# Splitting the output projection's weight of a decode block into nine groups, six of them gathered with different partitions left out

## The chip, the cores and the metric

The kernel runs on one core of one Trainium2 chip. The metric is device time in microseconds (us) of one execution; the number that counts is the median of several runs. Everything below that is called a profile or a trace is one profiled execution of the same program.

## What is computed

The reference is one decode step of a transformer block: two tokens (B = 2, one position each, D = 512), attention over a cache of 8192 keys and values for 32 heads of 128, and an MLP.

```python
# x [2,1,512]; k_cache, v_cache [2,32,8192,128]; wq [512,4096]; wo [4096,512]; w1 [512,1792]; w2 [1792,512]
q = layernorm(x) @ wq                       # 32 heads of 128
p = softmax(q . k_cache * 128**-0.5)        # per token and head, over 8192 positions
o = p . v_cache                             # [2, 32*128]
h = x + o @ wo
out = h + gelu(layernorm(h) @ w1 + b1) @ w2 + b2
```

The two caches are 268 MB each in float32 and are read once. All other operands together are about 25 MB; `wo`, which the change is about, is 8.4 MB.

## The kernel before

**Units of work.** Two heads of one token make a unit: 32 units, `i = 0 .. 31`, where unit `i` is head pair `m = i // 2` and token `b = i % 2`. A unit has one tile of keys and one of values, 4 MB each: 128 partitions (64 for each head) by 128 positions by 128 values. The tiles come from one pool, `kv`, with three buffers, in the order k0, v0, k1, v1, ..., so the load of `v_i` has to wait until `k_(i-1)` is used up, and that of `k_(i+1)` until `v_(i-1)` is. All these loads are issued by SyncE (SP), in that order (L65).

**One unit.** The scores are made in four chunks. VectorE (DVE) multiplies the key chunk by the query in place (L219, 4.4 us each), then sums part of the rows (L227), while ScalarE (ACT) sums the others (L223). After the fourth chunk `row_max` takes the largest score of each partition (L231), TensorE (PE) turns it, and at the start of the next unit `all_max` finds the largest of each head (L238, tile `gm`). From it ACT makes the exponentials (L254), and PE multiplies them with the values (L279). So DVE's work on unit `i` ends with the `gm` instruction, and the next thing on its queue is the first multiply of unit `i + 1`, which needs the keys `k_(i+1)`.

**The output projection.** `wo` of the first 30 heads, 3840 rows of 2 KB, is used in groups. A group is a tile `wog` of 128 partitions by 4 rows (`wts` pool, one buffer), loaded ahead by `load_wo`. `head_out` scales the finished head outputs and lays them out as the tile `orow` asks (L314), `turn` transposes that on PE (L322), `turned` copies it (L329, DVE) and multiplies it with `wog` into `rowacc` (L331, PE). The next group is loaded in the unit after that (`free_from`). The last two heads have their own load and path at the end.

**Two ways to load a group.** A plain group fills all 128 partitions with one DMA issued by SP (L125). A gathered group has 448 rows, 112 runs of 4 rows. GpSimd (POOL) fills the tile with zeros (L129) and issues an indirect DMA (L130) with one index for each partition; the partitions in `SHUT` get an index beyond the bounds and are left out. Before, there are four gathered groups, all with the same 16 partitions left out, and then four plain ones.

**The indices.** They are worked out on DVE, one set for each distinct tuple of blocks:

```python
index = {}
for blocks in SHUT:
    if blocks not in index:
        acc = work.tile([P, 1], F32, name="ixf")
        nc.vector.tensor_copy(acc, part)
        for s0 in blocks:
            for edge, step in ((s0, FAR), (s0 + 4, -FAR - 4)):
                one = work.tile([P, 1], F32, name="ix1")
                ...
        index[blocks] = const.tile([P, 1], I32, name="ix")
        nc.vector.tensor_copy(index[blocks], acc)      # L112
```

**What orders the work.** The tile framework keeps the order of each engine's queue near the order in the code (a few places say `behind(...)`), and adds the waits. A pool gives every name its own buffers, `const` one for each name, `work` two, `kv` three. A tile that is allocated under a name again takes the buffer of an earlier one, after what last used that one.

Of the kernel before, what the change touches and what calls it, by code (L numbers as in the profile page):

```python
# [16 lines left out]
P = 128  # L17
# [6 lines left out]
WARM = 3  # L24
WR = 4

SHUT = [(0, 4, 32, 36)] * 4
FAR = 4096


# [1 line left out]
def tile_decode_block(ctx: ExitStack, tc: tile.TileContext, x, k, v, wq, wo, w1, b1, w2, b2, out):  # L32
    nc = tc.nc
    B, H, SK, DH = k.shape
    D = x.shape[-1]
# [40 lines left out]
    def next_of_pool(make):  # L76
        with tc.issue_after(pool[0].ins):
            pool[0] = make()
# [2 lines left out]


    HL = H - QG
    GR = (P - 16) * WR
    groups = [(GR * g, GR, WR) for g in range(len(SHUT))]
    at = groups[-1][0] + GR
    while at < HL * DH:
        r = min(WR, (HL * DH - at) // P)
        groups.append((at, r * P, r))
        at += r * P  # L90
    kept = [[p for p in range(P) if g >= len(SHUT) or not any(s <= p < s + 4 for s in SHUT[g])]
            for g in range(len(groups))]
    group_end = {}
    for g, (r0, n, r) in enumerate(groups):
        group_end.setdefault((r0 + n - 1) // (QG * DH), []).append(g)

    part = const.tile([P, 1], F32, name="part")
# [1 line left out]
    next_of_pool(lambda: nc.gpsimd.iota(parti, [[0, 1]], base=0, channel_multiplier=1))  # L99
    nc.vector.tensor_copy(part, parti)  # L100
    index = {}
    for blocks in SHUT:
        if blocks not in index:
            acc = work.tile([P, 1], F32, name="ixf")
            nc.vector.tensor_copy(acc, part)
            for s0 in blocks:
                for edge, step in ((s0, FAR), (s0 + 4, -FAR - 4)):
                    one = work.tile([P, 1], F32, name="ix1")
                    nc.vector.tensor_scalar(one, part, edge - 0.5, float(step), op0=ALU.is_ge, op1=ALU.mult)
                    nc.vector.tensor_add(acc, acc, one)  # L110
            index[blocks] = const.tile([P, 1], I32, name="ix")
            nc.vector.tensor_copy(index[blocks], acc)  # L112
# [4 lines left out]
    wo_runs = wo.rearrange("(m r) n -> m (r n)", r=WR)  # L117
    wo_g = {}

    def load_wo(g, gate=None):  # L120
        r0, n, r = groups[g]
        t = wts.tile([P, WR, D], F32, name="wog")
        wo_g[g] = t
        if g >= len(SHUT):
            nc.sync.dma_start(t[:, :r], wo[r0:r0 + n, :].rearrange("(p r) n -> p r n", r=r))  # L125
            return
        if gate is not None:
            next_of_pool(lambda: nc.gpsimd.tensor_copy(gate0, gate))
        next_of_pool(lambda: nc.gpsimd.memset(t, 0.0))  # L129
        next_of_pool(lambda: nc.gpsimd.indirect_dma_start(  # L130
            t.rearrange("p r n -> p (r n)"), None, wo_runs, bass.IndirectOffsetOnAxis(index[SHUT[g]], 0),
            element_offset=r0 * D, bounds_check=P - 17, oob_is_err=False))

    epst = const.tile([P, 1], F32, name="epst")
    nc.vector.memset(epst, EPS)
# [167 lines left out]

    def head_out(h):
        rl = RL[h // QG * B + B - 1][:, h % QG:h % QG + 1]
        for g, (r0, n, r) in enumerate(groups):
            a, end = max(r0, h * DH), min(r0 + n, (h + 1) * DH)
            while a < end:
                q = (a - r0) // r
                run = 1  # L310
                while a + run * r < end and kept[g][q + run] == kept[g][q] + run:
                    run += 1
                c0, p0 = a - h * DH, kept[g][q]
                nc.vector.tensor_scalar(orow[g % 2][:B, :r, p0:p0 + run].rearrange("b r p -> b p r"),  # L314
                                        OP[h // QG][:, h % QG, c0:c0 + run * r].rearrange("b (p r) -> b p r", r=r),
                                        rl, None, op0=ALU.mult)
                a += run * r

    def turn(g):
        TP[g] = psm.tile([P, WR, B], F32, name="sm")  # L320
        for r in range(groups[g][2]):
            nc.tensor.transpose(TP[g][:, r, :], orow[g % 2][:B, r, :], ident[:B, :B])  # L322
        if g + 2 < len(SHUT) and SHUT[g + 2] != SHUT[g]:
            next_of_pool(lambda: nc.gpsimd.memset(orow[g % 2][:B], 0.0))

    def turned(g):
# [18 lines left out]
    for i in range(NI):  # L345
# [24 lines left out]
        if next_load < len(groups) and i == free_from:  # L370
            load_wo(next_load, MX[i - 1][:1, 0:1] if next_load == 0 else None)
            next_load += 1
            free_from = NI
        for c in range(NC):
            if i > 0 and c == 0:
                with behind(last):
                    mul = multiply(i, c)
            else:
                mul = multiply(i, c)
            ended = [g for g in group_end.get(done // B, ())] if done >= 0 and done % B == B - 1 else []  # L380
            with behind(mul):
                if i > 0 and c == 1:
                    inverse(done)
                if i > 0 and c == 2 and done % B == B - 1:
                    for h in range(done // B * QG, done // B * QG + QG):
                        head_out(h)
                if c == 3:
                    for g in ended:
                        turned(g)
                        free_from = i + 1  # L390
            by_act(i, c)
            if i > 0 and c == 0 and not late:
                gather(done)
            by_dve(i, c)
            if i > 0 and c == 0:
                total(done)
            if i > 0 and c == 1 and not late:
                head_sum(done)
            if c == 2:
                for g in ended:  # L400
                    turn(g)
# [154 lines left out]
```

## Time and profile before

| what | value |
|---|---|
| median of three runs | 1315.71 us (1313.37 to 1316.23) |
| the profiled execution: its own time | 1317.28 us |
| its span, first to last instruction | 1315.5 us |
| DMA: moved in all, mean rate | 561.67 MB, 427 GB/s |
| DVE busy | 971.2 us, 74% of the span |
| ACT busy | 479.4 us, 36% |
| PE busy | 459.0 us, 35% |
| POOL busy | 12.8 us, 1%, 18 instructions |
| granted TensorE clock, mean | 0.662 |

The span is what the views of the trace count in; the execution's own time is 1.8 us longer, and 1.6 us above the median. The page gives busy time for each engine, the DMA share in 40 slices, the chain of work that ended last, and groups of instructions by line. A timeline line reads: start, time from there to the end of the last instruction in the line, engine, line, operation, tile written and tiles read, count, and in brackets how long the engine sat idle before it and what ended that. L12 is line 12 of the kernel. In the changed kernel the lines named here are one higher (L112 becomes L113, L219 becomes L220).

### The profile page before, as it was taken

To read this page: it belongs to the slowest core of one execution; us is meant where nothing else is said; L and a number is where in the kernel's file an instruction comes from. 1 tells how busy PE (TensorE), PEld (TensorE's weight loads), DVE (VectorE), ACT (ScalarE), POOL (GpSimd) and SP (SyncE) were. 2 spreads that over 40 slices of the span, in tenths; PEclk is the share of its full clock that TensorE was granted. 3 is DMA by queue.
4 is the path that set the end of the run, shared out by engine and by line. 5 is a ranking of instruction groups with operands and counts; after the bars stand their busy time and mean duration, and the time that the engine had idled before them with its cause. 6 is when DMAs were issued, how large, how long until landed. Compare 5 with 4: busy or idle time off the path is not lost.

```text
span 1315.5 us, 10328 instructions
## 1 busy us (share of the span) xinstructions
PE 459.0 (35%) x3231; PEld 147.0 (11%) x3231; DVE 971.2 (74%) x447; ACT 479.4 (36%) x2955; POOL 12.8 (1%) x18
## 2 busy tenths in 40 slices
PE   3024213342332324313442332424412244323438
PEld 0001001110110101001010010101001011011104
DVE  1766788767788676788776788767688677798991
ACT  0333344433344333344333344333344333344441
POOL 0000000000000000000000000000000000000000
PEclk9566557766666667656766566766657676556758
DMA  9999999999999999999999999999999999999996
GB/s 415 443 417 441 422 439 439 423 437 430 433 435 425 439 431 429 431 430 437 431 427 437 435 427 435 425 439 435 425 437 430 435 433 425 439 423 423 442 415 263
DMA packets 13470, 561.67 MB, mean 427 GB/s; under 512 B 1556, under 2 KB 1572, under 8 KB 2984
## 3 DMA queue, kind: packets, MB, share of 16 engines
q1 hardware_dynamic: 12828, 557.34, 98.3%
q0 software_dynamic: 576, 3.67, 0.7%
q8 instruction: 25, 0.41, 0.1%
q14 instruction: 29, 0.24, 0.0%
q10 hardware_dynamic: 12, 0.01, 0.0%
HBM read 561.53 MB, written 0.00 MB: 427 GB/s over the span
## 4 chain that ended last, share of the span: by engine, by line
DMA 44%; DVE 32%; PE 17%; issue 6%; ACT 1%; POOL 0%; DVEq 0%; SPq 0%; POOLq 0%
DMA kv<-in_A_k_cache_dram 44%; DVE kv L219 21%; PE so L279 11%; DVE s L227 9%; PE rowacc L331 4%; ACT pt L254 1%; DVE orow L314 1%; PE so L501 0%; PE sm L242 0%; PE po L524 0%; PE sm L234 0%; DVE gm L238 0%; PE sm L484 0%; DVE mx L231 0%; ACT nb L248 0%
## 5 line engine op out<-in xcount | busy, mean ns | idle before, releaser
L219 DVE TENSOR_TENSOR kv<-kv,qps 128x4096 f32<-128x4096 f32 x128 | 560.7, 4411 | 277.5 <-DMA kv<-in_A_k_cache_dram 277.5
L223 ACT ACTIVATE kv<-kv 128x128 f32<-128x128 f32 x1376 | 403.9, 295 | 335.3 <-DVE kv L219 335.3
L227 DVE TENSOR_REDUCE s<-kv 128x20 f32<-128x2560 f32 (+2 forms) x128 | 377.7, 2972 | 0.3
L279 PE MATMUL so<-kv,pt 128*8 128x512 f32 x2048 | 284.3, 713 | 55.1 <-ACT pt L254 36.5
L223 ACT ACTIVATION_READ_ACCUMULATOR kv<-kv 128x1 f32 x1376 | 256.7, 187 | 0.0
L234 PE MATMUL sm<-ident,mx 128*1 128x128 f32 x32 | 11.1, 346 | 315.5 <-DVE mx L231 315.5
L285 ACT ACTIVATE ss<-so 128x512 f32<-128x512 f32 x32 | 19.1, 597 | 280.0 <-PE so L279 149.7
L204 PE MATMUL qps<-q,pick 2*64 2x128 f32 x128 | 16.7, 409 | 283.6 <-DVE kv L219 283.6
L279 PEld LDWEIGHTS so<-kv,pt 128*8 128x8 f32 x2048 | 58.3, 101 | 250.6 <-issue 208.7
L248 ACT ACTIVATE nb<-sm 128x1 f32<-128x1 f32 x32 | 5.5, 171 | 169.1 <-PE sm L242 169.1
L331 PE MATMUL rowacc<-wog,ot 128*2 128x512 f32 x64 | 47.4, 911 | 52.7 <-issue 27.1
L300 PE MATMUL sm<-ss,selr 128*2 128x128 f32 x480 | 55.8, 275 | 0.7 <-ACT ss L285 0.7
L204 PEld LDWEIGHTS qps<-q,pick 2*64 2x64 f32 x128 | 10.9, 202 | 297.4 <-DVE kv L219 274.4
L322 PE MATMUL sm<-ident,orow 2*128 2x2 f32 x32 | 4.5, 241 | 105.1 <-DVE orow L314 105.1
L300 PEld LDWEIGHTS sm<-ss,selr 128*2 128x2 f32 x480 | 39.2, 85 | 13.7 <-ACT ss L285 1.7
L234 PEld LDWEIGHTS sm<-ident,mx 128*1 128x1 f32 x32 | 2.5, 79 | 332.1 <-issue 287.5
L238 DVE TENSOR_REDUCE gm<-sm 1x2 f32<-1x128 f32 x32 | 8.9, 279 | 30.8 <-PE sm L234 30.8
L254 ACT ACTIVATE pt<-s,nb 64x128 f32<-64x128 f32 x64 | 25.5, 399 | 1.6 <-ACT nb L248 0.2
L331 PEld LDWEIGHTS rowacc<-wog,ot 128*2 128x2 f32 x64 | 6.6, 111 | 86.2 <-issue 60.3
L322 PEld LDWEIGHTS sm<-ident,orow 2*128 2x128 f32 x32 | 4.0, 209 | 107.3 <-issue 78.8
L242 PE MATMUL sm<-gm,srow 1*64 1x1 f32 x128 | 11.2, 238 | 11.5 <-DVE gm L238 11.5
L191 PE MATMUL so<-wqs,yT 128*2 128x512 f32 x64 | 9.2, 742 | 15.0 <-DMA wqs<-in_A_wq_dram 15.0
(100 smaller groups left out, 126.1 us busy)
## 6 DMA issues: line engine op xcount, KB each, us to landing
kv<-in_A_k_cache_dram SPq DMA_DIRECT2D x4, 4096.0 KB
kv<-in_A_k_cache_dram SPq DMA_DIRECT2D x4, 2048.0 KB, 26.5
wog<-in_A_wo_dram SPq DMA_DIRECT2D x4, 1024.0 KB, 36.3
kv<-in_A_v_cache_dram SPq DMA_DIRECT2D x1, 4096.0 KB, 36.0
ws<-in_B_w_dram SPq DMA_DIRECT2D x4, 896.0 KB, 10.8
kv<-in_A_v_cache_dram SPq DMA_DIRECT2D x1, 2048.0 KB, 40.5
ws<-in_B_w_dram SPq DMA_DIRECT2D x2, 1024.0 KB
kv<-in_A_v_cache_dram SPq DMA_DIRECT2D x1, 1536.0 KB
```

Source lines behind the costliest of these rows:

```text
L204: nc.tensor.matmul(qps[m][e * HP:(e + 1) * HP, b], pick[32 * n:32 * n + B, b, :], q2[32 * n:32 * n + B, at + e * DH:at + (e + 1) * DH], st ...
L219: return nc.vector.tensor_tensor(kc, kc, qb, op=ALU.mult)
L223: nc.scalar.activation(kt[i][:, j, :], kt[i][:, j, :], AF.Copy, accum_out=ST[i][:, j:j + 1])
L227: return nc.vector.tensor_reduce(ST[i][:, a:e], kt[i][:, a:e, :], axis=AX.X, op=ALU.add)
L234: nc.tensor.transpose(MT[i], mx, ident)
L242: nc.tensor.matmul(GM[i][e * HP:(e + 1) * HP], srow, gm[:, e:e + 1], start=True, stop=True)
L254: nc.scalar.activation(ptz[i % 2][ps, :, 4 * e:4 * e + 4], s[ps], AF.Exp, bias=nb[ps], scale=SCALE, accum_out=LT[m][ps, b:b + 1])
L279: m = nc.tensor.matmul(so[32 * n:32 * n + 4 * QG], ptz[i % 2][:, u, :], vt[i][:, 4 * u:4 * u + 4, :], start=(u < NG), stop=(u >= NS // 4 - ...
L285: return nc.scalar.activation(SS[i], so2[i % 2], AF.Copy)
L300: nc.tensor.matmul(OP[m][:, e, :], sel_row[:, c, 4 * e + j, :], SS[i - 1 + c][:, j * DH:(j + 1) * DH], start=(c == 0 and j == 0), stop=(c ...
L314: nc.vector.tensor_scalar(orow[g % 2][:B, :r, p0:p0 + run].rearrange("b r p -> b p r"), OP[h // QG][:, h % QG, c0:c0 + run * r].rearrange( ...
L331: nc.tensor.matmul(rowacc, t[:, r, :], wo_g[g][:, r, :], start=False, stop=(g == len(groups) - 1 and r == n - 1))
```

## The change

`SHUT`, four equal tuples, is replaced by `PLAN`, nine entries. The first is one head, 128 rows, as a plain load with one row for each partition. Then come six gathered groups of 448 rows; the first two leave out the same 16 partitions as before, and the other four each leave out another choice of four blocks of four partitions. Two plain groups of 512 rows (four heads) end the list. The row count is still 3840.

There are five distinct tuples now, so the loop over `index` runs its body five times, and allocates `ix` five times. Where the group that will use the same half of `orow` leaves out other partitions, `turn` issues a memset of that half on POOL; before, that condition never held. The groups end in other head pairs, so the loads and the products with `wo` move to other units: the gathers are issued at the start of units 3, 7, 9, 13, 17 and 21 (before 1, 5, 9 and 13), the plain loads in units 1, 23 and 27 (before 15, 19, 23 and 27).

```diff
-SHUT = [(0, 4, 32, 36)] * 4
+PLAN = [1, (0, 4, 32, 36), (0, 4, 32, 36), (4, 12, 20, 36), (4, 24, 36, 68), (4, 36, 72, 76), (80, 84, 88, 92), 4, 4]
...
-    GR = (P - 16) * WR
-    groups = [(GR * g, GR, WR) for g in range(len(SHUT))]
-    at = groups[-1][0] + GR
-    while at < HL * DH:
-        r = min(WR, (HL * DH - at) // P)
-        groups.append((at, r * P, r))
-        at += r * P
+    groups, at = [], 0
+    for blocks in PLAN:
+        shut = blocks if isinstance(blocks, tuple) else None
+        r = WR if shut else blocks
+        n = (P - 4 * len(shut or ())) * r
+        groups.append((at, n, r, shut))
+        at += n
...
-    for blocks in SHUT:
-        if blocks not in index:
+    for _, _, _, blocks in groups:
+        if blocks and blocks not in index:
...
     def load_wo(g, gate=None):
-        r0, n, r = groups[g]
+        r0, n, r, shut = groups[g]
         t = wts.tile([P, WR, D], F32, name="wog")
         wo_g[g] = t
-        if g >= len(SHUT):
+        if not shut:
             nc.sync.dma_start(t[:, :r], wo[r0:r0 + n, :].rearrange("(p r) n -> p r n", r=r))
             return
...
         next_of_pool(lambda: nc.gpsimd.indirect_dma_start(
-            t.rearrange("p r n -> p (r n)"), None, wo_runs, bass.IndirectOffsetOnAxis(index[SHUT[g]], 0),
-            element_offset=r0 * D, bounds_check=P - 17, oob_is_err=False))
+            t.rearrange("p r n -> p (r n)"), None, wo_runs, bass.IndirectOffsetOnAxis(index[shut], 0),
+            element_offset=r0 * D, bounds_check=n // r - 1, oob_is_err=False))
...
-        if g + 2 < len(SHUT) and SHUT[g + 2] != SHUT[g]:
+        if g + 2 < len(groups) and groups[g + 2][3] and groups[g + 2][3] != groups[g][3]:
             next_of_pool(lambda: nc.gpsimd.memset(orow[g % 2][:B], 0.0))
```

More of the change, by code (lines that the diff above doesn't have):

```diff
@@ L83, in tile_decode_block @@
     HL = H - QG
-    GR = (P - 16) * WR
-    groups = [(GR * g, GR, WR) for g in range(len(SHUT))]
-    at = groups[-1][0] + GR
-    while at < HL * DH:
-        r = min(WR, (HL * DH - at) // P)
-        groups.append((at, r * P, r))
-        at += r * P
-    kept = [[p for p in range(P) if g >= len(SHUT) or not any(s <= p < s + 4 for s in SHUT[g])]
-            for g in range(len(groups))]
+    groups, at = [], 0
[5 more added lines that the diff above has]
+        at += n
+    assert at == HL * DH
+    kept = [[p for p in range(P) if not any(s0 <= p < s0 + 4 for s0 in shut or ())] for _, _, _, shut in groups]
     group_end = {}
-    for g, (r0, n, r) in enumerate(groups):
+    for g, (r0, n, r, _) in enumerate(groups):
         group_end.setdefault((r0 + n - 1) // (QG * DH), []).append(g)
@@ L305, in head_out @@
         rl = RL[h // QG * B + B - 1][:, h % QG:h % QG + 1]
-        for g, (r0, n, r) in enumerate(groups):
+        for g, (r0, n, r, _) in enumerate(groups):
             a, end = max(r0, h * DH), min(r0 + n, (h + 1) * DH)
```

## The prediction

> **What bounds the kernel now.** I read the page's slices and its chain first, then the queue's own waits, then the timeline around one gather.
>
> ```profile
> DMA  9999999999999999999999999999999999999996
> DMA 44%; DVE 32%; PE 17%; issue 6%; ACT 1%; POOL 0%; DVEq 0%; SPq 0%; POOLq 0%
> L219 DVE TENSOR_TENSOR kv<-kv,qps 128x4096 f32<-128x4096 f32 x128 | 560.7, 4411 | 277.5 <-DMA kv<-in_A_k_cache_dram 277.5
> ```
>
> All sixteen DMA engines are busy in 39 of 40 slices. DVE, the next in line, idles 277.5 us, all of it in front of a unit's first multiply, for keys. So bytes set the time, as long as the next load is issued before the engines run dry. Who issues it is seen in the waits of SP's own queue:
>
> ```profile
> SPq L65 <- DVE s L227: 827.4, 31, 38.7
> ```
>
> SP waits 827.4 us for the last sum (L227) of a unit: that frees the key buffer for the next values. DVE therefore sets when half of the loads start; it merely does so early enough. How early, the timeline shows around the second gather of before, a place like the ones the change touches (DVE, then POOL, then SP):
>
> ```profile
> 226.87 0.15 DVE L329 COPY ot<-sm 128x8 f32<-128x8 f32 x1
> 233.49 0.28 DVE L238 TENSOR_REDUCE gm<-sm 1x2 f32<-1x128 f32 x1 [2.50 <-PE sm L234]
> 239.57 8.75 DVE L219 TENSOR_TENSOR kv<-kv,qps 128x4096 f32<-128x4096 f32 x2 [5.81 <-DMA kv<-in_A_k_cache_dram]
> 269.50 0.28 DVE L238 TENSOR_REDUCE gm<-sm 1x2 f32<-1x128 f32 x1 [0.56 <-PE sm L234]
> 280.80 4.42 DVE L219 TENSOR_TENSOR kv<-kv,qps 128x4096 f32<-128x4096 f32 x1 [11.02 <-DMA kv<-in_A_k_cache_dram]
> ```
> ```profile
> 233.32 1.80 POOL L129 MEMSET wog<- 128x2048 f32 x1 [158.07 <-PE rowacc L331]
> 235.39 1.00 POOL L130 DMA_INDIRECT wog<-in_A_wo_dram,ix  x1 [0.27 <-POOL wog L129]
> ```
> ```profile
> 230.66 0.33 SPq L65 DMA_DIRECT2D kv<-in_A_v_cache_dram  x1
> 244.21 0.33 SPq L65 DMA_DIRECT2D kv<-in_A_k_cache_dram  x1
> 268.62 0.33 SPq L65 DMA_DIRECT2D kv<-in_A_v_cache_dram  x1
> ```
>
> DVE ends a unit at 233.77, idles 5.81 us, works from 239.57 to 269.78, idles 11.02. Values are issued at 268.62, and the engines have the keys before them in work until about 280.8. The gather goes out at 235.39, just behind DVE's `gm`. Its landing, from the answer on line L130:
>
> ```profile
> L130 POOL DMA_INDIRECT wog<-in_A_wo_dram,ix x4: 995/996/1175, 74.1 to 550.6; - x4
> DMA to landing us min/median/max: 26.3/26.7/27.4
> ```
>
> **The change part by part.**
>
> *Bytes.* 3840 rows as before: no change.
>
> *The index buffer, which decides.* `ix` is one name in a pool with one buffer for a name. Before, it was allocated once. Now there are five sets, and each must wait until the gathers with the set before it have landed. The built order of DVE's queue in the changed kernel says where it waits:
>
> ```
> L239 TensorReduce gm<-sm 1x2
> L113 TensorCopy ix<-ixf 128x1 [waits for two gathers' landings]
> L106, L111, L110 ... 17 more index operations
> L220 TensorTensor kv<-kv,qps 128x4096
> ```
>
> The copy stands between `gm` and the first multiply of a unit, four times: units 7, 9, 13 and 17, each the unit at whose start POOL issues the very gather (third to sixth entry of the plan) that the copy waits for. 17 operations are behind it the first time, 15 the second, none later. Behind them are queued the unit's multiplies and sums; for these wait ACT's sums, the exponentials, PE's values, and SP's next values.
>
> One stall, from the rows: `gm` ends at 233.77; issue 235.39 plus 26.7 is 262.1. The index operations cost 0.09 us each (27 small DVE operations between 5.45 and 8.18 at the start, 0.28 of that idle), so 18 cost 1.6 us, 16 cost 1.4 and a lone copy 0.15. DVE multiplies at 263.7, 263.5 and twice 262.2, where it would at 239.57: 24.1, 23.9, 22.7 and 22.7 us late. Spare is 280.80 - 268.62 = 12.2 us, less the time from issue to the first packet: the last DMA, issued at 1312.49, moves its first bytes in the stretch 1313.5 to 1314, so 1.0 to 1.5, taken 1.2, and less up to 0.5 between a landing and the multiply, taken 0.3. That leaves 10.7. The engines stand still 13.4 + 13.2 + 12.0 + 12.0 = 50.6 us. In the unit after a stall DVE works without idling (29 to 30 us against 38.7 between keys), so it has caught up before the next one two units later. Bounds: a gather of 26.3 and spare of 11.0 give 48; 27.4 and a spare of 7.6 (unit 17 of before, without a gather beside it: values issued 745.20, multiply 754.47) give 51 + 2.8 + 12.4 = 66.
>
> *Instruction fetches, no longer paid for.* The page has 25 instruction packets on one queue and 29 on another. In the trace's packets most of the latter fall on one of the two engines that carry no gather packets: leaving out its partitions made up for them. By the ends of its loads it goes from 4.4 us ahead of the median engine, behind the last gather, to 1.8 behind it at the last values: 6.2 us in 673. Each stall ends with all engines idle, so its lead is lost; behind the last stall some 545 us of loads follow, 5.0 us. Bounds 0 (hidden by the others' lag) and 10 (the same between stalls): 5.
>
> *Balance.* What the other blocks would gain shows in the last packets: the DMA share is 0.14 in 1305 to 1306 and 0.07 in 1306 to 1307, one engine working alone. Perfect balance would end at about 1305.2, so 0 to 2 us, and after the stalls nothing: 0.
>
> *More POOL and DVE work.* Six gathers for four, five memsets of `orow` (at most the 1.80 us of L129), 46 scalings at L314 for 36 (0.40 us each, 4 us in all, at most 6 of them in a unit). DVE idles (277.5 - 34.2) / 30 = 8.1 us in a mean unit and covers them; in a stalled unit (7, 9, 13, 17, all of the second token) there are no scalings. Of the 72 added index operations 36 are counted in the stalls, and 36 stand at the start, where DVE idles 34.2 us before its first keys. 0.
>
> *SP.* One plain load of 256 KB comes early, two plain ones go; all stand right behind a key load and wait for nothing new. 0.
>
> Sum: 50.6 + 5 = 56, on the execution's own 1317.3: 1373; the median lies 1.6 lower: 1372.
>
> **A rule against this.** The traced gather took 26.7 us, because each of its 8 KB packets takes its turn with 64 KB ones. The Trainium skill (DMA: Bandwidth & Descriptors, section Anatomy of one DMA) fits 2.0 us plus bytes over 436 GB/s for a DMA from GpSimd; for 0.92 MB that is an estimate of 4.1 us, and the stall would be hidden. The trace disagrees, 26.7 against 4.1, since the queue beside it is full; it weighs only as the second rival.
>
> **The rivals.** *The whole lag is passed on (7%).* If DVE and ACT cannot catch up between stalls, each costs its full 22.7 to 24.1: 93 us, 1409. For it: two stalls lie only two units apart. Against: 8.1 us idle in a mean unit, so that a lag of 24.1 - 10.7 = 13.4 us passed to the engines costs once and isn't added to. *The gather lands before the multiply is due (7%), the other side.* Place: the copy behind `gm`. Price: nothing, if the landing comes less than 5.81 + 10.7 = 16.5 us behind `gm`, that is, within 15 us of the issue. Then only the balance is left: 1314 to 1316. For it: fewer packets for some engines. Against: the slowest engine still has all eight, and all four landings of before lie within 26.3 and 27.4. The change not doing what it says would be the same case.
>
> **How the numbers follow.** The stalls hold 86%, likeliest 1372. Their bounds are 1315.7 + 48 + 0 = 1364 and 1315.7 + 66 + 10 = 1392; the low end is taken down to 1359, since each standstill also levels the engines and may give back 1 us or so, and the high end to 1390, all upper bounds at once being unlikely. 1359 to 1390 holds about 8 in 10. Within 0.2% of before (2.6 us, what a measurement can tell from no change) are most of the second rival, 5%; faster 2%; slower 93%.
>
> **What would show it.** In the profile after, DVE idle in front of L113 four times by about 28 us (262.1 - 233.77), ended by the gather's landing; the DMA digits fall below 9 in four slices, at units 8, 10, 14 and 18; DVE's idle time before L220 shrinks by about as much as L113 shows; bytes unchanged. Wrong it would be if the copy found its gather landed, if the gather became quicker beside an emptier queue, or if the engines' standstill were made up later, which bytes at a full rate don't allow.

## The result, and the profile after

The changed kernel takes 1371.92 us (median of four runs, 1370.45 to 1374.34), the kernel before 1314.62 (four runs, 1313.37 to 1316.23): a ratio of 1.0436, 95% interval 1.0419 to 1.0452. It is slower by 57 us; the forecast was 1372. The profiled execution took 1374.34 us with a span of 1372.6, against 1317.28 and 1315.5 before.

The page of the changed kernel, its slices, the first line of its chain and two of its groups (busy time and mean, then the idle time in front and what ended it):

```profile
DMA  9999999999599599996999969999999999999996
DMA 43%; DVE 35%; PE 12%; issue 8%; ACT 1%; POOL 1%; SPq 0%; DVEq 0%; POOLq 0%
L220 DVE TENSOR_TENSOR kv<-kv,qps 128x4096 f32<-128x4096 f32 x128 | 560.7, 4411 | 214.6 <-DMA kv<-in_A_k_cache_dram 214.6
L113 DVE CAST ix<-ixf 128x1 int32<-128x1 f32 x5 | 0.8, 154 | 114.3 <-DMA wog<-in_A_wo_dram,ix 114.3
```

Four slices of the DMA row fall to 5 or 6, where there was a 9 before. And a new group is in the table: five copies of one index column, 0.8 us of work, with 114.3 us of idle time in front of four of them, all ended by the gather into `wog`. How one of these comes about is seen in the timelines of the changed kernel around unit 7, DVE first (start, time to the end, line; in brackets the idle time before):

```profile
311.35 0.28 DVE L239 TENSOR_REDUCE gm<-sm 1x2 f32<-1x128 f32 x1 [2.02 <-PE sm L235]
340.08 0.15 DVE L113 CAST ix<-ixf 128x1 int32<-128x1 f32 x1 [28.45 <-DMA wog<-in_A_wo_dram,ix]
...
342.28 8.75 DVE L220 TENSOR_TENSOR kv<-kv,qps 128x4096 f32<-128x4096 f32 x2
...
372.22 0.28 DVE L239 TENSOR_REDUCE gm<-sm 1x2 f32<-1x128 f32 x1 [0.56 <-PE sm L235]
372.43 8.73 DVE L220 TENSOR_TENSOR kv<-kv,qps 128x4096 f32<-128x4096 f32 x2
```

Then POOL, and SP's queue:

```profile
313.25 1.00 POOL L131 DMA_INDIRECT wog<-in_A_wo_dram,ix  x1 [0.27 <-POOL wog L130]
```
```profile
320.37 0.33 SPq L66 DMA_DIRECT2D kv<-in_A_k_cache_dram  x1
371.34 0.33 SPq L66 DMA_DIRECT2D kv<-in_A_v_cache_dram  x1
```

The gather is issued at 313.25 and lands 26.8 us later. DVE waits for it with a copy that belongs to a later set, and starts unit 7 at 342.28. Its keys were there long before: with a buffer for each set (below) the same unit starts at 317.73, when they land. Unit 7's last sum, and with it SP's next values, comes at 371.34. In this kernel's windows (after the two times: length, busy time of PE, weight load, DVE, ACT and POOL, the granted clock, the DMA share, GB/s) the engines have then long run dry:

```profile
350.00:400.00 50.00, 16.17 (x117) 6.27 (x118) 49.34 (x21) 23.92 (x156) 0.52 (x1) 0.64 0.70 296
358.00:368.00 10.00, 1.12 (x8) 0.72 (x8) 10.00 (x4) 5.48 (x36) 0.00 (x0) 0.50 0.00 0
450.00:500.00 50.00, 16.05 (x124) 6.13 (x128) 45.45 (x23) 21.27 (x133) 0.00 (x0) 0.64 0.75 319
600.00:650.00 50.00, 13.26 (x96) 4.35 (x96) 42.40 (x16) 15.67 (x99) 0.00 (x0) 0.56 0.76 321
750.00:800.00 50.00, 7.05 (x64) 1.65 (x64) 22.52 (x7) 12.39 (x79) 1.44 (x2) 0.60 0.88 379
800.00:850.00 50.00, 25.15 (x180) 7.79 (x180) 38.25 (x19) 17.54 (x109) 0.00 (x0) 0.65 0.88 376
```

From 358 to 368 not a byte moves, while DVE works all the time. The five long windows lack 0.30, 0.25, 0.24, 0.12 and 0.12 of 50 us (the fourth standstill lies across 800): 51.5 of the 57 us.

The trace's single packets say it closer. The times in which none of the sixteen engines had a packet, the standstills, are 13.9 us from 358.4, 10.5 from 454.7, 11.4 from 625.3 and 11.1 from 796.5: 46.9 us, and none before. A standstill starts when the slowest engine is done; the others were done earlier. In the 8 us up to the four standstills the mean engine had already been without a packet for 1.5, 1.8, 1.7 and 1.6 us, and in the 5 us after each for 0.2 more. It therefore lost more than the standstills: from the first loads to the last (the mean of the sixteen engines' ends) it was 55.3 us longer without a packet than before, 8.4 more than 46.9. It also spent 2.9 us more in packets, and the tail behind the last loads was 1.2 us shorter. That adds up to the 57.1 us between the two spans. (Some packets overlap, so the mean engine's time without one comes out at -1.2 us before and 54.1 after; only differences are used here.)

### The profile page after: what moved, and what is told of

The parts are those of the page before. It is cut to its first block, busy times and chain, and to the rows that moved or that the text cites. A ratio compares the mean times of both kernels' runs of the same rounds, so it can differ in the third digit from the quotient of the medians.

```text
span 1372.6 us, 10433 instructions
## 1 busy us (share of the span) xinstructions
PE 457.3 (33%) x3234; PEld 146.6 (11%) x3234; DVE 979.6 (71%) x528; ACT 479.0 (35%) x2955; POOL 20.8 (2%) x26
## 2 busy tenths in 40 slices
DMA packets 13615, 561.68 MB, mean 409 GB/s; under 512 B 1604, under 2 KB 1620, under 8 KB 3160
## 4 chain that ended last, share of the span: by engine, by line
DMA 43%; DVE 35%; PE 12%; issue 8%; ACT 1%; POOL 1%; SPq 0%; DVEq 0%; POOLq 0%
DMA kv<-in_A_k_cache_dram 32%; DVE kv L220 22%; DVE s L228 11%; PE so L280 9%; DMA wog<-in_A_wo_dram,ix 8%; DMA kv<-in_A_v_cache_dram 3%; PE rowacc L332 1%; ACT pt L255 1%; DVE orow L315 1%; POOL wog L130 1%; PE so L502 0%; PE sm L235 0%; PE po L525 0%; PE sm L243 0%; PE sm L485 0%
## 5 line engine op out<-in xcount | busy, mean ns | idle before, releaser
L220 DVE TENSOR_TENSOR kv<-kv,qps 128x4096 f32<-128x4096 f32 x128 | 560.7, 4411 | 214.6 <-DMA kv<-in_A_k_cache_dram 214.6
L286 ACT ACTIVATE ss<-so 128x512 f32<-128x512 f32 x32 | 19.1, 597 | 282.1 <-PE so L280 150.3
L113 DVE CAST ix<-ixf 128x1 int32<-128x1 f32 x5 | 0.8, 154 | 114.3 <-DMA wog<-in_A_wo_dram,ix 114.3
L243 PE MATMUL sm<-gm,srow 1*64 1x1 f32 x128 | 11.1, 237 | 11.5 <-DVE gm L239 11.5
```

What stands on the lines that cost most here:

```text
L220: return nc.vector.tensor_tensor(kc, kc, qb, op=ALU.mult)
L286: return nc.scalar.activation(SS[i], so2[i % 2], AF.Copy)
```

## The experiments

The theory: `ix` has one buffer, so each new index set waits for a gather that was issued a moment ago, and the wait stands on DVE's queue in front of a unit's first multiply. The rivals that were put against it: the other blocks of partitions, or the groups' new places, slow the loads themselves; a second buffer would be enough; a gather takes 27 us whatever runs beside it, so that its own length is not to be helped.

**A buffer for each set.**

```diff
-            index[blocks] = const.tile([P, 1], I32, name="ix")
+            index[blocks] = const.tile([P, 1], I32, name=f"ix{len(index)}")
```

> The changed kernel with a name, and so a buffer, for each of the five index sets; all else as changed. Theory (the copy into the one index buffer holds up DVE): no idle time in front of L113, no standstill of the DMA engines, 1312 to 1317 us, that is 55 to 60 below the changed kernel; the other blocks left out may gain 0 to 2 us on the kernel before. Rival (the time lies in the groups themselves, six gathers and five memsets on POOL, or 46 scalings on DVE): 1365 to 1375 us, as these stay.

1314.16 us (12 runs, 1310.74 to 1315.97), against 1315.37 of the kernel before (23 runs): 0.9988 [0.9977, 0.9998]. On the page of this kernel, and in the answer on line L113:

```profile
DMA  9999999999999999999999999999999999999997
L220 DVE TENSOR_TENSOR kv<-kv,qps 128x4096 f32<-128x4096 f32 x128 | 560.8, 4411 | 267.3 <-DMA kv<-in_A_k_cache_dram 267.3
```
```profile
L113 DVE CAST ix<-ixf x5: 153/153/155, 8.0 to 15.5; 128x1 int32<-128x1 f32 x5
```

All five copies are done between 8.0 and 15.5 us, ahead of the first keys. The gathers land as late as in the changed kernel (26.1 to 27.1 us), and nobody waits for them. One name takes away 57.8 us (the two kernels were not run side by side; against the kernel before beside each, 4.4% becomes nothing). The new plan itself, with its six gathers, other blocks and other places, is worth a gain of 0.1%, hardly more than the interval, which lies just below 1.

**One set for all six gathers.**

```diff
-PLAN = [1, (0, 4, 32, 36), (0, 4, 32, 36), (4, 12, 20, 36), (4, 24, 36, 68), (4, 36, 72, 76), (80, 84, 88, 92), 4, 4]
+PLAN = [1, (0, 4, 32, 36), (0, 4, 32, 36), (0, 4, 32, 36), (0, 4, 32, 36), (0, 4, 32, 36), (0, 4, 32, 36), 4, 4]
```

> The nine groups of the changed kernel, but all six gathers leave out the same sixteen partitions as before, so there is one index set. Theory: no rewrite, no stall, within 3 us of the kernel before; against five buffers it shows what the choice of blocks is worth, 0 to 2 us in favour of the other blocks. Rival (more gathers and other groups cost the time): 1365 to 1375 us.

1314.87 us (11 runs), 0.9996 [0.9986, 1.0005]: no stall, no difference. Between this and the kernel with five buffers lie 0.7 us, and their intervals overlap: what the choice of blocks is worth can't be told from nothing. With this run and the one above, the rival of slower loads falls.

**The kernel before, with nothing but rewrites.** The groups of before, but the same set is worked out anew for each of the four gathers, into the one buffer. Against the kernel before:

```diff
-    for blocks in SHUT:
-        if blocks not in index:
+    for n, blocks in enumerate(SHUT):
+        if True:
...
-            index[blocks] = const.tile([P, 1], I32, name="ix")
+            index[n] = const.tile([P, 1], I32, name="ix")
...
```

> The kernel before with its own groups and blocks, and only the index set worked out anew for each of its four gathers into the one buffer: three copies, which wait for the gathers of units 1, 5 and 9. Theory (the rewrite alone does it): three stalls, 9 us at unit 1 and 11 to 14 at units 5 and 9, with the lag of the slowest engine 1350 to 1360 us. Rival (it takes the changed groups): 1312 to 1318 us.

1359.99 us (4 runs, 1356.94 to 1361.23): 1.0329 [1.0307, 1.0351]. On its page:

```profile
DMA  9996999969999599999999999999999999999996
L112 DVE CAST ix<-ixf 128x1 int32<-128x1 f32 x4 | 0.6, 154 | 85.2 <-DMA wog<-in_A_wo_dram,ix 85.2
```

Four sets give three rewrites: three idles, three dips, standstills of 10.7, 11.4 and 11.2 us. The bytes, the blocks and the gathers' places are those of before. So the rewrite alone makes the loss, about 15 us for each.

**Two buffers.**

```diff
-            index[blocks] = const.tile([P, 1], I32, name="ix")
+            index[blocks] = work.tile([P, 1], I32, name="ix")
```

> The changed kernel with two buffers for the index sets in place of one (the pool with two buffers for a name); all else as changed. In the built order the first two sets are written at the start; the copies of the third, fourth and fifth wait for the gathers of units 7, 9 and 13, which are issued at the start of just these units. Theory: three stalls, at units 7, 9 and 13, and the one at unit 17 gone: 1314 + 3 x 14 = 1356 us (1351 to 1361). Rival (a second buffer is enough, as it is for other tiles): 1312 to 1317 us.

1357.63 us (4 runs, 1356.04 to 1359.95): 1.0313 [1.0295, 1.0331]. On its page:

```profile
DMA  9999999999599699995999999999999999999996
L113 DVE CAST ix<-ixf 128x1 int32<-128x1 f32 x5 | 0.8, 154 | 85.3 <-DMA wog<-in_A_wo_dram,ix 85.3
```

The second buffer saves one stall of four, not the other three. The third set must wait until both gathers of the first set have landed, and its copy stands right behind the second of them, in unit 7; the set isn't needed before unit 13. By the landing after 26.8 us, a place one unit later in the queue would have found the gather landed; that was not tried. The rival that a second buffer is enough falls.

**One rewrite, early and late.** Two sets with the same partitions left out in another order, so that only the rewrite is new, apart from one or two memsets of 0.5 us on POOL; first in unit 7, then in unit 17 (each in place of the PLAN with one set):

```diff
+PLAN = [1, (0, 4, 32, 36), (0, 4, 32, 36), (32, 36, 0, 4), (32, 36, 0, 4), (32, 36, 0, 4), (32, 36, 0, 4), 4, 4]
```
```diff
+PLAN = [1, (0, 4, 32, 36), (0, 4, 32, 36), (0, 4, 32, 36), (0, 4, 32, 36), (0, 4, 32, 36), (32, 36, 0, 4), 4, 4]
```

> As with one set, but the last four gathers name the same sixteen partitions in another order, which makes one second index set: one copy, at unit 7. Theory: one stall, 13 to 17 us above one set (the first standstill of the changed kernel, 13.9 us, and up to 2 us for the lag of the slowest engine). If the whole lag of DVE were passed on: 24 us. Rival (several sets cost nothing): as one set.

> As with one set, but only the sixth gather has the second index set: one copy, at unit 17. Theory: one stall, 11 to 15 us above one set (the last standstill of the changed kernel, 11.1 us, 1.7 us for the lag of the slowest engine, and up to 2 us because the engine that fetches instructions has only one gather left that spares it). If a stall's price did not add up from stall to stall, early and late would differ from a quarter of the 57 us by more than 4 us. Rival: as one set.

Early: 1325.90 us (6 runs, 1325.09 to 1330.41), 1.0086 [1.0071, 1.0101], 11.0 us above the kernel with one set. Late: 1330.17 (4 runs, 1329.79 to 1330.51), 1.0114 [1.0099, 1.0128], 15.3 above it. The early one is below what was expected, the late one above it by 0.3 us. The stall is the same in both; from DVE's timelines, first of the early one, then of the late one:

```profile
339.55 0.15 DVE L113 CAST ix<-ixf 128x1 int32<-128x1 f32 x1 [28.26 <-DMA wog<-in_A_wo_dram,ix]
```
```profile
735.77 0.15 DVE L113 CAST ix<-ixf 128x1 int32<-128x1 f32 x1 [28.27 <-DMA wog<-in_A_wo_dram,ix]
```

Each has one standstill of 11.3 us, and up to the last loads the mean engine lost 13.0 and 14.0 us without a packet against the kernel with one set. What is left of the difference lies behind the last loads: from there to the end it took 5.8 us in the early kernel's trace, 8.8 in the late one's and 9.5 with one set. Just ahead of that stretch, while the last loads still run, PE works at a clock that changes from one moment to the next:

```profile
1310.00:1315.00 5.00, 5.00 (x59) 1.71 (x51) 0.70 (x5) 1.75 (x3) 0.00 (x0) 0.75 0.99 412
```
```profile
1310.00:1315.00 5.00, 5.00 (x46) 2.58 (x49) 0.66 (x4) 1.16 (x2) 0.00 (x0) 0.50 1.01 421
```

In the windows of these two (early, late; the clock is the number ahead of the DMA share) PE is busy all 5 us in both, granted 0.75 in the one and 0.50 in the other. That this clock is why the tails differ is argued from one trace each, not shown. Nor does the tail belong to early or late: two traces of the changed kernel itself (the second is from the last experiment) have 9.0 and 6.9 us there, and one of the six early runs took 1330.41, as long as the late ones.

**A shorter gather.** The loads of keys and values in half the size, two DMAs for a tile, their packets 32 KB where they were 64. The index buffer stays one. The same with five buffers is the control.

```diff
-                vt[i] = load(v, i, cut(1))
+                vt[i] = load(v, i, cut(2))
...
-            kt[i + 1] = load(k, i + 1, parts_of.get(i + 1, cut(1)))
+            kt[i + 1] = load(k, i + 1, parts_of.get(i + 1, cut(2)))
```

> The changed kernel with the key and value loads up to unit 29 in two DMAs each, so that a packet beside the gather is 32 KB in place of 64. Theory (a gather's 8 packets for each engine take turns with the load's, so it lands in about 4 + 8 x (1.22 + 0.31) = 16 us in place of 26.8): DVE idle in front of L113 about 18 us, each standstill 10 us shorter, 1 to 4 us in place of 11 to 14: 1318 to 1335 us. Rival (the landing takes 26 to 27 us whatever the packets beside it, as by a fixed cost on GpSimd's queue): 1365 to 1375 us.

> Control for the half packets: the same two DMAs for each load, with five index buffers. Both: as with five buffers and whole packets, 1311 to 1318 us; what it differs from that is the price of the smaller packets.

With one buffer 1320.82 us (10 runs, 1317.55 to 1322.16), 1.0036 [1.0025, 1.0046]; the control 1316.52 (10 runs, 1315.09 to 1320.32), 1.0015 [1.0002, 1.0028]. So the four rewrites, 57.8 us in the changed kernel, cost 4.3 here. From the first kernel's answer on line L131, its page, and its timeline of DVE in unit 7:

```profile
DMA to landing us min/median/max: 16.5/17.3/17.5
```
```profile
DMA  9999999999999999999999999999999999999996
L113 DVE CAST ix<-ixf 128x1 int32<-128x1 f32 x5 | 0.8, 154 | 74.7 <-DMA wog<-in_A_wo_dram,ix 74.7
```
```profile
302.96 0.28 DVE L239 TENSOR_REDUCE gm<-sm 1x2 f32<-1x128 f32 x1 [2.52 <-PE sm L235]
321.44 0.15 DVE L113 CAST ix<-ixf 128x1 int32<-128x1 f32 x1 [18.20 <-DMA wog<-in_A_wo_dram,ix]
323.67 8.75 DVE L220 TENSOR_TENSOR kv<-kv,qps 128x4096 f32<-128x4096 f32 x2
```

The gather of the same 0.92 MB lands after 17.3 us instead of 26.8. That fits packets that take turns with packets half as long: eight gather packets on an engine, each beside a packet of 1.22 us instead of 2.42 (medians in the traces), would save 9.6 us, and 9.5 are saved. DVE still idles 74.7 us in front of L113, but the longest single idle is 19.1 us, and at no time do all engines stand still. So the loss goes with the gather's length, and an idle time counts only as far as it goes beyond the spare. By the spare of before, a multiply 16.5 us behind `gm`, unit 7 should even here have stood still for about 4 us (323.67 less 303.24 less 16.5). With halved loads the spare is therefore larger as well, so that the two were not taken apart, and why it is larger was not tried. The spans of the two traces differ by 5.8 us, against 4.3 between the medians: 2.2 before the end of the last loads and 3.6 behind it, in the same tail as above; where they come from stays open.

**The lost lead.** The prediction gave 5 us to an engine that loses its lead at every standstill. Here the sixth gather leaves out the first set's blocks in another order, so that the spared engines are those of the first two gathers. There are still five sets and four stalls. The changed kernel ran again beside it.

```diff
-PLAN = [... (80, 84, 88, 92), 4, 4]
+PLAN = [... (36, 32, 4, 0), 4, 4]
```

> The changed kernel, but the sixth gather, the one behind the last stall, leaves out the first sixteen partitions again (named in another order, so that there are still five sets and four stalls). Theory of the instruction fetches (behind the last stall one engine falls behind the others, 4.8 us by the last loads, as it fetches instructions and no gather spares it): that engine is spared 8 packets of 0.31 us, 2.5 us, while the twelve to sixteen others carry theirs; the last data come 1 to 2.5 us earlier, the time is 1 to 2 us below the changed kernel run beside it. If the lag does not matter for the end: no difference (within 0.7 us).

> The changed kernel itself, beside the one with the last gather's blocks altered: 1369 to 1375 us by every theory; it is the reference for that one.

1371.22 us (5 runs, 1366.32 to 1372.75) against 1374.13 (5 runs, 1372.91 to 1374.43); to the kernel before, 1.0422 [1.0399, 1.0444] and 1.0446 [1.0431, 1.0461]. The two intervals overlap, but all five times lie below all five of the changed kernel; the medians are 2.9 us apart, where 1 to 2 were expected. The packets agree: when the keys of unit 29 land, the slowest engine is 4.9 us behind the median one in the changed kernel and 1.3 here. The mean engine has 3.2 us less without a packet, but about half of that lies ahead of the altered gather, where the two kernels do the same: the first standstill is 12.6 us here and 14.7 there. Behind the last standstill the mean engine is done with its loads after 553.1 us here, and after 555.8 and 555.9 in the two traces of the changed kernel. So there is such a term behind the last stall, and it is of about 3 us.

## Why the prediction was right

**Bytes: right.** 561.68 MB for 561.67.

**The index buffer: right, 50.6 us forecast, 46.9 measured.** The four idles in front of L113 are 28.45, 28.96, 28.50 and 28.39 us, where about 28 was said, each ended by the gather issued in that unit. The gathers took 26.3 to 27.3 us, as before. The index operations behind the copies were priced a little low: from the copy's start to the multiply 2.2 us in place of 1.6 the first time, 2.0 in place of 1.4 the second. The standstills of 13.9, 11.4 and 11.1 us lie within 1 us of 13.4, 12.0 and 12.0. The second, 10.5 for 13.2, is the one mis-sized term here: the spare was taken as 10.7 everywhere, and two units behind a stall it is larger. In unit 7 the engines run dry 46.8 us after `gm` ends (358.4 less 311.6), in unit 9 50.4 (454.7 less 404.3), in the other two 47.2 and 47.4; with two buffers, too, the standstill of unit 9 is the shortest, 8.8 us beside 13.4 and 12.2. DVE had run the unit between without idling, so it was further ahead of the loads than usual; that this is the reason is read from the timelines, not tried. The prediction used it only to rule out a passed-on lag. (In its upper bound the spare of 7.6 should be 7.8: 754.47 less 745.20, less the same 1.5. That makes 65 of 66.)

**Instruction fetches: the lag came as said, but a term beside it was missing.** The sum has 5 us for one engine's lost lead at the end, and what came beside the standstills is about 10 (57.1 less 46.9). The engine's lag itself is there, 4.9 us by the keys of unit 29; sparing that engine was worth about 3. The missing term is the uneven finish at each standstill. The text even held that a standstill might give back 1 us or so by levelling the engines. It is the other way round: the slowest engine sets the start of a standstill, and the rest have waited for it. In the changed kernel that makes 6.7 us ahead of the four standstills and 0.8 right behind them, 7.5 of the 8.4. In the mean engine's time without packets, less the standstills, each stall cost 2.1 us more in the changed kernel (8.4 over four), 2.3 with rewrites in the kernel before, about 2 with two buffers, 1.7 and 2.7 with one rewrite. The 2.9 us more in packets have no term either; the rewrites alone bring them to the kernel before as well (2.9), and their cause stays open. The sum of 56 came within 1 us by luck: the two misses, 3.7 too much and 5 too little, nearly cancel.

**Balance, the further POOL and DVE work, SP: right at nothing.** With the wait taken away the plan's remainder is -1.2 us against the kernel before, within the 0 to 2 that the last packets gave for balance. (The scalings were 44, not 46; the largest number in a unit is 6, as said.)

**The rule weighed against the forecast.** The Trainium skill (DMA: Bandwidth & Descriptors, section Anatomy of one DMA) would give an estimate of 4.1 us for this gather. The runs measure 26.8 beside packets of 64 KB and 17.3 beside packets of 32 KB: the landing went with the size of the packets in the other queue. The measurements decide, and the second rival, which needed a landing within 15 us, did not come about in the changed kernel.

**The first rival** (the whole lag passed on, 1409) is out as well: the standstills are half of its 93 us.

**What would show it.** Idles, four dips and bytes were as said. One sign was wrong: DVE's idle time in front of L220 was to shrink by about as much as L113 shows. It shrank by 62.9 us (277.5 to 214.6) for 114.3. It couldn't be otherwise: what DVE loses and the loads don't make good reappears as a longer span, and the prediction's own 50.6 should have been taken off.

## What to carry to other kernels

A tile name with one buffer is a wait, and its price depends on where the scheduler puts the rewrite: look in the built order for a small instruction that waits on a DMA's landing and stands in front of the engine's main work. Price it as the lateness it causes less the spare of the loads behind that engine, and add the uneven finish of the DMA engines, 2 us a time here. A constant made once for each variant wants a name of its own: four index columns of 512 bytes saved cost 4% here.

## What the runs showed of the hardware that was not expected

- A gather's landing went by the packet size of the other queue: 26.8 us beside 64 KB packets, 17.3 beside 32 KB ones, for the same 0.92 MB. Halving the packets cost about 2 us in itself (1316.52 against 1314.16, both with five buffers, on two chips that differ by 0.4 us for the kernel before).
- The wait was not proportional to its cost. Four idles of 18.7 us on average cost 4.3 us in all, four of 28.6 cost 57.8.
- Two kernels with the same standstill of 11.3 us, one early and one late, differ by 4.3 us. In their traces most of it lies behind the last loads, and PE's granted clock was between 0.50 and 1.00 around there. Two traces of one and the same kernel differ by 2.2 us in that stretch. The cause was not settled.
